# Two-layer spectral and MLP mixer on one core: fewer opening matmuls, a gate ahead of a GpSimd step, and a rewritten order of layer 2

## The chip, the core and the metric

The kernel runs on one core of a Trainium2 chip. The core's engines work side by side, each through its own queue in order: TensorE (PE, matmuls; its weight loads are listed as PEld), VectorE (DVE), ScalarE (ACT), GpSimd (POOL) and SyncE (SP, which here only starts DMAs). They wait for one another through semaphores. Matmuls write to PSUM, which has eight banks of 128 x 512 fp32; DVE or ScalarE have to evict a result before its bank can be written again. The metric is device time in microseconds (us); lower is better.

## What is computed

```python
def reference(x, w_r, w_i, w1, w2, w3, w4):      # names shortened, B = 1, S = 2048, D = 512, F = 1792
    for _ in range(2):                           # the same two blocks twice
        x = x + A(layernorm(x))
        x = x + Bk(layernorm(x))
    return x

def A(x):                                        # global filter
    X = rfft2(x)                                 # over S and D
    return irfft2(X * (w_r + 1j * w_i), s=(S, D)).astype(bf16)

def Bk(x):                                       # spatial shift + MLP
    h = gelu(layernorm(x) @ w1)
    # quarter c of the columns is shifted by -1, +1, -2, +2 rows, zeros moving in
    x1 = x + shift(h) @ w2
    return x1 + gelu(layernorm(x1) @ w3) @ w4
```

Everything is bf16 in and out, with fp32 sums.

## The kernel before

The 2048 rows are split as s = 16 p + q: p on the 128 partitions, q as sixteen row blocks of 128 x 512. The whole state x stays in SBUF. The two-dimensional FFT is done as small matrix products, in this sequence: over p (`over_p`, with a table T that is scaled per row block by the layer norm's 1/std, called Tq), over the columns d (`over_d`), over q (`over_q`, with the table TL), then the product with the filter W (`weigh`, on DVE), and back over q (`back_q`, with the table TR), d (`back_d`) and p (`back_p`). The q transforms of the sixteen frequency groups b need TL in two forms, of which only the first is loaded; the second is made on the chip by swapping and negating columns (`turn_TL`, L227, two GpSimd operations for each half of the table). W is loaded for half of the partitions and doubled by DMAs from SBUF to SBUF (L183); TR's third plane is a negated copy of its first (`negate`, L759, on DVE).

The order of all work is written out by hand, as strings of short codes: ORDER_0 for the first p transforms, ORDER_A for layer 1 and ORDER_B for layer 2. Each code issues the instructions of one step, and each engine runs its share in the order in which the codes stand. A number after the dot is the PSUM bank. In the layers:

- d, t: d transform and its eviction to TV; q, x: q transform and its eviction to X; p: the product with W
- b, m: back over q and its eviction to hT; D, Y: back over d and its eviction; P, a: back over p and the add into x, with a row sum
- s, r, e, i, c, n: squares, statistics and the normalizing of rows for the MLP; T: the DMA transpose of two row blocks (SP queue)
- v, h: w1 matmuls and gelu; u, f: w2 matmuls and the add of the shifted rows; k, R, o: second norm; U: its DMA transposes
- w, g: w3 matmuls and gelu (ScalarE, 128 x 1024 at a time); W, A: w4 matmuls of a row block (14 of them) and the add into x; y: the store of a row block (SP queue)
- a letter V or A after the number of t, x, m, Y, n or o says whether DVE or ScalarE does it.

In ORDER_0, Q scales T for a row block (letter V: DVE, A: ScalarE), O is a p transform of one or two row blocks, and G its eviction to V. The row blocks come in the order 2, 3, 0, 1, 6, 7, 4, 5, 10, 11, 8, 9, 13, 12, 14, 15; the last tables are Q13V Q12V, Q14V and Q15A.

At the very start PE runs WAKE matmuls on a tile of zeros (`wake`, L241, `fill`, L252) while x is loaded; a few more zero matmuls stand between the first p transforms (FILL). `load_rest` (L179) is called once after ORDER_0 has been issued and fills GpSimd's queue: the loads of FA, TL and half of TR, the first doubling of W, the turn of TL's first half, the second doubling, the turn of the second half, two more doublings, and the other half of TR. Nothing in it waits for the p transforms. `load_mlp` (L199) puts the loads of the MLP weights on SP's queue; its first DMA reads what the last doubling wrote.

Layer 2 ends with the stores. In layer 1 one row block (row 14 of the order, `columns`, L688) has its w4 matmuls, add and statistics done in two column halves of 256, numbered 14 and 24; all other row blocks, and all of layer 2's, are done in one piece of 512 columns. `store` (L707) writes whole row blocks.

The instructions go out through a framework that places each engine's waits from the tiles that are read and written; the order strings are kept as they stand.

Of the kernel before, what the change touches and what calls it, by code (L numbers as in the profile page):

```python
# [13 lines left out]
BF16 = dt.bfloat16  # L14
# [4 lines left out]
D = 512  # L19
# [134 lines left out]
def load_all(K, A_x, A_w_r, A_w_i, B_w1, B_w2, B_w3, B_w4):  # L154
    nc = K.nc
    tabs = dft_tables()
    dram = {k: nc.inline_tensor(v, name="tab_" + k).ap() for k, v in tabs.items()}

    def table(k, eng):
        t = K.const.tile(list(tabs[k].shape), BF16, name=k)  # L160
        eng.dma_start(t[:], dram[k])
        setattr(K, k, t)

    K.x = K.big.tile([P, NQ, D], BF16, name="x_state")
    xv = A_x[0].rearrange("(p q) d -> p q d", q=NQ)
    table("T", nc.scalar)
    for h in range(8):
        nc.sync.dma_start(K.x[:, h * 2:h * 2 + 2, :], xv[:, h * 2:h * 2 + 2, :])
    K.W = K.const.tile([P, 2, NH, 257], BF16, name="W")
    planes = [w.rearrange("(m j) f -> m j f", j=64) for w in (A_w_r, A_w_i)]  # L170
    for pl, v in enumerate(planes):
        nc.scalar.dma_start(K.W[2::4, pl, 0], v[:, 32])
    for lo in range(0, NH, 8):
        for pl, v in enumerate(planes):
            load_W(K, v, pl, lo, lo + 8)
    K.TL = K.const.tile([P, 2, NB, P], BF16, name="TL")
    K.TR = K.const.tile([P, 3, NH, 64], BF16, name="TR")

    def load_rest():  # L179
        q = nc.gpsimd  # L180
        load_TL = lambda k: q.dma_start(K.TL[:, 0, 8 * k:8 * k + 8], dram["TL"][:, 8 * k:8 * k + 8])
        load_TR = lambda k: q.dma_start(K.TR[:, 0:2, 16 * k:16 * k + 16], dram["TR"][:, :, 16 * k:16 * k + 16])
        double = lambda k: q.dma_start(K.W[1::2, :, 8 * k:8 * k + 8], K.W[0::2, :, 8 * k:8 * k + 8])  # L183
# [12 lines left out]
    K.load_rest = load_rest
    K.load_G2 = lambda: nc.sync.dma_start(K.G[:], dram["G2"])

    def load_mlp():  # L199
        gate2 = K.const.tile([1, 16], BF16, name="gate2")  # L200
        nc.sync.dma_start(gate2[:], K.W[1:2, 1, NH - 1, 1:17])
        for k in ("G", "Tinv"):
            table(k, nc.sync)
        for k, w, n, c in (("w1", B_w1, 4, D), ("w2", B_w2, 4, D), ("w3", B_w3, 4, FH), ("w4", B_w4, 14, D)):
            t = K.const.tile([P, n, c], BF16, name=k)
            nc.sync.dma_start(t[:], w.rearrange("(t p) n -> p t n", p=P))
            setattr(K, k, t)

    K.load_mlp = load_mlp
    K.eps = K.const.tile([P, 1], FP32, name="eps")  # L210
    nc.vector.memset(K.eps[:], EPS)
    K.eps2 = K.const.tile([P, 1], FP32, name="eps2")
    nc.gpsimd.memset(K.eps2[:], EPS * EPS)
    K.mhalf = K.const.tile([P, 4], FP32, name="mhalf")
    nc.gpsimd.memset(K.mhalf[:], -0.5)
# [11 lines left out]
def turn_TL(K, sl):  # L227

    old, new = [K.TL[:, k, sl].rearrange("p b (c h) -> p b c h", h=2) for k in range(2)]
    K.nc.gpsimd.tensor_scalar(new[:, :, :, 0], old[:, :, :, 1], -1.0, None, op0=ALU.mult)  # L230
    K.nc.gpsimd.tensor_copy(new[:, :, :, 1], old[:, :, :, 0])
# [9 lines left out]
def wake(K):  # L241
# [6 lines left out]
    K.zeros = t  # L248
    fill(K, WAKE)

# [120 lines left out]
def scaled_T(K, q, r, eng="V"):  # L371

    K.Tq[q] = K.stream.tile([P, 2, P], BF16, name="Tq", bufs=12)
    if eng in "VP":
        e = K.nc.vector if eng == "V" else K.nc.gpsimd
        e.tensor_scalar(K.Tq[q][:], K.T[:], r, None, op0=ALU.mult)
    else:
        K.nc.scalar.activation(K.Tq[q][:], K.T[:], ACT.Copy, bias=0.0, scale=r)
# [51 lines left out]
def first_front(K):  # L430

    new_V(K)
    K.Tq = {}
    at = {q: (g, i) for g, rows in enumerate(GROUPS) for i, q in enumerate(rows)}
    L = [Stats(K, n=len(rows)) for rows in GROUPS]
    for g, rows in enumerate(GROUPS):
        if any(q in ON_ACT for q in rows):
            L[g].sums()
    ps = {}

    def stats(q):
        g, i = at[q]
        if q in ON_ACT:
            L[g].mean(i, K.x[:, q, :])
            L[g].square(i, K.x[:, q, :])
        else:
            L[g].bn(i, K.x[:, q, :])

    def aggr(q):
        g, i = at[q]  # L450
        L[g].aggr(i)

    def scale(q, eng):
        g, i = at[q]
        scaled_T(K, q, L[g].r[:, i:i + 1], eng)

    def front(k):
        ps[k] = over_p(K, FIRST[k], k == len(FIRST) - 1)
        if k in FILL:
            fill(K, FILL[k])  # L460

    def take(k, eng):
        take_V(K, FIRST[k], ps[k], eng, k == len(FIRST) - 1)

    def means(g):
        for i, q in enumerate(GROUPS[g]):
            if q in ON_ACT:
                L[g].from_means(i)

    table = {"s": stats, "i": aggr, "f": means, "S": lambda g: L[g].std(),  # L470
             "J": lambda g: L[g].invert(), "p": lambda g: L[g].rstd(), "Q": scale, "O": front, "G": take}
    for op in ORDER_0.split():
        if op[0] in "QG":
            table[op[0]](int(op[1:-1]), op[-1])
        else:
            table[op[0]](int(op[1:]))
    K.load_rest()
    K.load_mlp()
    spare = K.grp.tile([P, 4, 4, P], BF16, name="xT", bufs=4)
    K.nc.sync.dma_start_transpose(spare[:, 0, 0:1], K.zeros[:])  # L480


def layer(K, last):
# [3 lines left out]
    nc = K.nc  # L487
# [114 lines left out]
    def rstd2(g):  # L602
        ln[g].from_sums()
        ln[g].rstd_twice(g in ROOT)
        if g not in ROOT:
            ln[g].shift()
# [80 lines left out]

    def columns(n):  # L688

        if last or n % 10 != 4 or n < 14:  # L690
            return n, slice(0, D)
        return 14, slice(0, D // 2) if n == 14 else slice(D // 2, D)

    def w4(n):
        r, d = columns(n)
# [9 lines left out]
        nc.vector.tensor_tensor(x, ps.pop(("W", n)), x, op=ALU.add)  # L705

    def store(n):  # L707
        nc.sync.dma_start(K.out_v[:, ROWS[n], :], K.x[:, ROWS[n], :])

    def stats4(n):  # L710
        r, d = columns(n)
# [73 lines left out]
            table[op[0]](int(op[1:]))  # L785


WAKE = 44
FILL = {0: 3, 1: 3, 2: 2, 3: 2, 4: 2}
GROUPS = [[0, 1, 2, 3], [4, 5, 6, 7], [8, 9, 10, 11], [12, 13], [14, 15]]  # L790
ON_ACT = [1, 5]
FIRST = [[0, 1], [2, 3], [4, 5], [6, 7], [8, 9], [10, 11], [12, 13], [14], [15]]
UNITS = {b: [b, b + 1] if 2 <= b < 14 else [b] for b in (0, 1, 2, 4, 6, 8, 10, 12, 14, 15)}
ROOT = (0, 1)
LATE = ((14, 15), (0, 14))
TAKE_B = ("FFFFFFFFFFFFFFFB", "FFFFFFFFFFFFFFFB")
ROWS = [*range(2, 16), 0, 1]
# [26 lines left out]
G6A G14A X4.5 X3.4 L6  # L824
"""
ORDER_B = """
d4.0 d1.3 d8.6 t4A q4.0 t1A q1.2 t8A x4V d15.5 t15A p4 d12.6 x1A p1 t12A d10.4 q15.0 x15A p15 t10A q8.2 x8V q12.6 x12A
d2.0 t2A d0.4 d14.5 b1.3 m1A q10.0 t0A q2.6 t14A p8 b8.3 x2A m8A d6.4 t6A p12 x10V b5.2 m5A p2 b12.1 m12A p10 b13.0
q0.4 m13V q6.6 x0A x6A q14.2 b4.1 m4A p0 b10.4 b11.5 p6 x14A m11A m10A b3.6 m3A b9.0 b0.1 m0A p14 m9V b7.2 m7V b2.7
b14.4 m14A b6.5 m2V b15.2 m6A m15V m15A D3.6 Y3A D2.0 Y2A D1.4 Y1A P6.6 a6 P4.1 P7.7 a4 s6 P5.5 a7 s4 D0.3 s7 a5 s5  # L830
D5.0 Y0V Y5A r1 e1 P3.6 a3 s3 P1.4 a1 i1 n6V s1 P0.7 a0 P2.6 a2 P10.2 P11.5 n7A D4.3 n5V s0 T3 s2 D6.0 n4V T2 D7.6 Y4V
Y6A P8.4 P13.1 r0 e0 Y7A a10 s10 i0 n0A n3V n2V T1 n1V a13 P12.3 P9.2 P14.7 a9 a11 s13 s9 a8 P15.0 a15 s11 s8 v2.1
v3.5 h3 a14 a12 r2 n10V h2 s15 T0 v1.4 h1 n11V n9V v0.6 T5 n8V u3.2 c1 f3 h0 u1.5 s12 u0.0 s14 c0 T4 f1 u2.7 v5.1 f0
E0 k0 r3 n12V k1 n13V v4.4 n15V n14V f2 h5 k3 u4.6 f4 h4 k2 u7.2 c2 f7 E3 R0 o3A u5.5 f5 u6.3 k7 T6 T7 E7 v6.4 h6 o0V
E2 E1 o1V U0 o2V U1 v7.6 h7 u13.1 k4 u12.2 E5 c3 f13 k13 f6 u15.6 E6 f15 u14.0 f12 E12 w5.3 g5 f14 k14 k12 E14 u11.2
f11 w2.6 w1.0 g1 k15 R3 g2 w3.4 w6.0 g3 u9.6 g6 f9 E15 w0.4 w4.6 g0 u8.2 E13 k5 o15V f8 E8 u10.4 f10 g4 W2.7 W1.4 k6
E10 o13V A2 o14A U7 R1 o12A U6 o6V E4 k11 W0.2 A0 A1 o5V k9 o4V U2 W3.0 A3 w26.3 g26 k10 w22.0 g22 w27.2 o7V y1 w21.5
w24.0 E11 g21 z0 y3 E9 g24 k8 R2 w23.6 g23 g27 o10V U3 w12.0 g12 o9V w25.4 g25 W13.3 A13 w10.0 g10 W12.6 A12 w8.4 o8V
W15.7 U4 g8 A15 w9.3 y12 g9 o11V U5 W14.0 w7.1 g7 w19.3 g19 w13.6 A14 y2 w17.4 g17 w11.0 g11 g13 W6.5 A6 y0 W4.7 A4
W5.0 A5 y13 w20.5 W7.4 g20 w14.2 g14 A7 w15.4 y4 g15 w16.0 g16 w18.5 g18 W9.2 A9 y7 W8.3 A8 W11.4 y15 A11 W10.7 A10 y5  # L840
y6 y14 y11 y9 y8 y10
"""


# [28 lines left out]
```

## Time and profile before

| | us |
|---|---|
| median of five runs (lowest to highest) | 349.68 (349.25 to 350.26) |
| the profiled run | 349.87 |
| its span from first to last instruction | 348.1 |
| PE busy in the span | 337.1 |
| ScalarE busy | 197.3 |
| DVE busy | 185.7 |
| GpSimd busy | 62.2 |

Most numbers in this text come from the timeline of one profiled execution, whose times count from the span's start. A row gives start, length, engine, line, operation, output and inputs, shapes, and a count where several equal instructions stand in a row; in brackets, idle time of the engine before it and what ended it. Lengths run from the start to the last write, and a following instruction of the same engine usually starts a little before that. A matmul's end is modelled: matmuls of 256 columns are listed with 0.27 us but follow each other every 0.109 us, and those of 512 columns every 0.216 us.

Where PE stands in the kernel, by its timeline: the zero matmuls from 1.01 us, the first p transform at 7.26, the first d transform at 18.82, layer 1's back transforms from about 30, layer 2's first d transform at 185.03, its D stage at 204.70, its w1 matmuls from 219.37, and the last w4 matmul just before the last add at 344.02.

### The profile page before, as it was taken

The numbers are of one execution on the slowest core, as the hardware profiler recorded it, in microseconds if no ns is written. First come the engines' busy times: TensorE is split into PE (matmuls) and PEld (weight loads), VectorE is DVE, ScalarE is ACT, GpSimd is POOL, SyncE is SP. The second block draws the span as 40 slices with busy tenths as digits, with TensorE's granted clock in tenths as the row PEclk, the third lists the DMA queues.
The fourth block names the chain that finished last, engine by engine and source line by source line (L and its number), as shares of the span: only waits on it lengthen the run. The fifth ranks groups of instructions, "written<-read, shape, count | busy, mean of one in ns | idle before, by whom it ended". The sixth has DMA issues, their size and how long they took to land. (4 is left out here: it accounts for less than half of the span.)

```text
span 348.1 us, 5562 instructions
## 1 busy us (share of the span) xinstructions
PE 337.1 (97%) x2110; PEld 188.7 (54%) x2129; DVE 185.7 (53%) x444; ACT 197.3 (57%) x350; POOL 62.2 (18%) x157
## 2 busy tenths in 40 slices
PE   8899999999999999999999999999999999999995
PEld 6668885444444444445577888544444444444442
DVE  5989597568424417844786969767343201102011
ACT  5969999864803706424528989985581372150410
POOL 2560046422200003200100002463130010000000
PEclk9999999999999999999999999999999999999999
DMA  7987956303030110400000002454003400400201
GB/s 245 289 291 216 370 159 118 74 19 61 1 62 0 28 34 0 90 2 0 1 2 0 2 2 43 82 107 77 0 2 60 90 0 15 108 0 17 75 0 60
DMA packets 45129, 24.38 MB, mean 70 GB/s; under 512 B 34928, under 2 KB 42096, under 8 KB 45104
## 3 DMA queue, kind: packets, MB, share of 16 engines
q1 hardware_dynamic: 43760, 20.00, 23.0%
q0 software_dynamic: 1104, 3.94, 3.2%
q8 instruction: 16, 0.26, 0.3%
q10 hardware_dynamic: 240, 0.10, 0.1%
q14 instruction: 9, 0.07, 0.1%
HBM read 11.41 MB, written 2.10 MB: 39 GB/s over the span
## 5 line engine op out<-in xcount | busy, mean ns | idle before, releaser
L686 ACT ACTIVATE gT<-ps 128x1024 bf16<-128x1024 f32 x56 | 56.4, 1022 | 103.3 <-PE ps L679 102.9
L679 PE MATMUL ps<-xT,w 128*128 128x512 bf16 x448 | 99.8, 379 | 0.2 <-DMA xT<-xn 0.2
L699 PE MATMUL ps<-w,gT 128*128 128x512 bf16 (+1 forms) x448 | 97.8, 372 | 0.6
L705 DVE TENSOR_TENSOR x_state<-ps,x_state 128x512 bf16<-128x512 f32 (+1 forms) x33 | 22.0, 674 | 97.7 <-PE ps L699 93.8
L699 PEld LDWEIGHTS <-gT 128*128 128x128 bf16 x462 | 45.1, 98 | 51.3
L679 PEld LDWEIGHTS <-w 128*128 128x128 bf16 x448 | 43.6, 98 | 52.8 <-issue 0.9
L652 DVE SCALAR_TENSOR_TENSOR xn<-xn,ln_c,ps 128x512 bf16<-128x512 bf16 x32 | 23.3, 744 | 25.0 <-PE ps L644 9.3
L644 PE MATMUL ps<-w,hT 128*128 128x512 bf16 x123 | 28.8, 379 | 0.3
L628 PE MATMUL ps<-xT,w 128*128 128x512 bf16 x128 | 28.6, 379 | 0.0
L596 DVE SCALAR_TENSOR_TENSOR x_state<-ps,x_state 128x512 bf16<-128x512 f32 x32 | 20.4, 685 | 7.1 <-PE ps L588 7.0
L282 ACT ACTIVATE junk<-xn 128x512 bf16<-128x512 bf16 x32 | 19.9, 622 | 5.9 <-DVE xn L652 5.7
L270 DVE BATCH_NORM_STATS2 ln_st<-x_state 128x6 f32<-128x512 bf16 (+1 forms) x31 | 20.0, 665 | 3.7 <-DMA x_state<-in_A_x_dram 3.5
L644 PEld LDWEIGHTS <-hT 128*128 128x128 bf16 x128 | 12.5, 98 | 15.4 <-ACT hT L635 0.4
L547 DVE TENSOR_TENSOR PB<-X,W 128x2048 bf16<-128x2048 bf16 (+1 forms) x20 | 20.2, 1050 | 0.5 <-ACT X L151 0.4
L628 PEld LDWEIGHTS <-w 128*128 128x128 bf16 x128 | 12.4, 98 | 14.9 <-issue 0.6
L282 ACT ACTIVATE xn<-x_state 128x512 bf16<-128x512 bf16 x32 | 20.0, 630 | 0.4
L635 ACT ACTIVATE hT<-ps 128x512 bf16<-128x512 f32 x32 | 17.6, 605 | 3.2 <-PE ps L628 2.9
L288 POOL TENSOR_SCALAR ln_mv<-ln_s 128x4 f32<-128x4 f32 x16 | 4.3, 269 | 77.1 <-DVE x_state L596 66.4
L151 ACT ACTIVATE TV<-ps 128x1024 bf16<-128x1024 f32 (+1 forms) x15 | 14.4, 981 | 3.6 <-PE ps L504 2.3
L504 PE MATMUL ps<-FA,V 128*128 128x256 bf16 x128 | 16.0, 273 | 0.3 <-ACT V L151 0.2
L305 POOL TENSOR_SCALAR ln_ve<-ln_mv 128x4 f32<-128x4 f32 x11 | 3.3, 302 | 71.8 <-DVE ln_mv L298 71.1
L576 PE MATMUL ps<-G,hT 128*128 128x256 bf16 x128 | 15.3, 273 | 0.8 <-ACT hT L151 0.4
(86 smaller groups left out, 392.1 us busy)
## 6 DMA issues: line engine op xcount, KB each, us to landing
w<-in_B_w_dram SPq DMA_DIRECT2D x2, 1792.0 KB, 13.8
W<-W POOLq DMA_DIRECT2D x4, 514.0 KB, 4.5
x_state<-in_A_x_dram SPq DMA_DIRECT2D x8, 256.0 KB, 5.2
out_dram<-x_state SPq DMA_DIRECT2D x16, 128.0 KB, 1.9
TR<-tab_TR POOLq DMA_DIRECT2D x2, 512.0 KB, 6.3
w<-in_B_w_dram SPq DMA_DIRECT2D x2, 512.0 KB, 5.8
W<-in_A_w_r_dram SPq DMA_DIRECT2D x7, 128.5 KB, 7.0
W<-in_A_w_i_dram SPq DMA_DIRECT2D x7, 128.5 KB, 6.6
```

Source lines behind the costliest of these rows:

```text
L270: self.K.nc.vector.bn_stats(self.st[i][:, int(k)], src)
L282: K.nc.scalar.activation(out, src, ACT.Square, bias=0.0, scale=D ** -0.5, accum_out=self.s[:, i, 1:2])
L547: nc.vector.tensor_tensor(t, X.pop(u)[:, 0:2 * n].unsqueeze(1).to_broadcast([P, 2, 2 * n, 256]), K.W[:, :, 2 * u:2 * u + 2 * n, 1:257], op ...
L596: nc.vector.scalar_tensor_tensor(K.x[:, q, :], ps.pop(("P", q)), 1.0, K.x[:, q, :], op0=ALU.mult, op1=ALU.add, accum_out=ln[g].s[:, i, 0:1])
L628: nc.tensor.matmul(o[:, i], lhsT=K.w1[:, t, j * P:(j + 1) * P], rhs=xT[g][:, :, t, :], start=(t == 0), stop=(t == 3))
L635: nc.scalar.activation(hv[:, 2 * h + i, 4 * g:4 * g + 4, PAD:PAD + P], o[:, i].rearrange("p (q c) -> p q c", q=4), ACT.Gelu_apprx_tanh, bi ...
L644: nc.tensor.matmul(o, lhsT=K.hT[:, j, st:st + P], rhs=K.w2[:, j, :], start=(j == 0), stop=(j == 3))
L652: nc.vector.scalar_tensor_tensor(xn[:, q, :], xn[:, q, :], ln[q // 4].c[:, q % 4:q % 4 + 1], ps.pop(("u", n)), op0=ALU.mult, op1=ALU.add, ...
L679: nc.tensor.matmul(o[:, i], lhsT=K.w3[:, c, t * P:(t + 1) * P], rhs=xT3[g][:, :, c, :], start=(c == 0), stop=(c == 3))
L686: nc.scalar.activation(gT[g][:, 2 * j:2 * j + 2, :], ps.pop(("w", k)), ACT.Gelu_apprx_tanh, bias=0.0, scale=1.0)
L699: nc.tensor.matmul(o, lhsT=gT[g][:, t, i * P:(i + 1) * P], rhs=K.w4[:, t, d], start=(t == 0), stop=(t == 13))
L705: nc.vector.tensor_tensor(x, ps.pop(("W", n)), x, op=ALU.add)
```

## The change

Four things change.

1. WAKE goes from 44 to 35.
2. `load_rest` takes the last scaled table as an argument, and GpSimd copies two elements of it to a small tile before it turns the first half of TL. As the queue is in order, everything behind that copy starts after the last table (row block 15's) has been written.
3. `columns` now halves one row block in each layer, HALVES = (14, 10): row 14 in layer 1 as before, row 10 in layer 2, numbered 10 and 20. `store` stores a half when it is given one.
4. ORDER_B is another string throughout. It contains the same steps, with W20, A20 and y20 added, in another sequence, with other banks, and with other engines for some evictions: t1 and x15 move from ScalarE to DVE; of the m, DVE has 10, 11, 14 and 7 instead of 13, 9, 7 and 2; Y3 and Y4 are on DVE instead of Y0 and Y4; n7 is on DVE instead of ScalarE; of the sixteen o steps, ten change their engine. The last w4 steps are W10.5, W9.7 and W20.0.

```diff
-    def load_rest():
+    def load_rest(after):
...
         double(0)
+        gate = K.const.tile([1, 2], BF16, name="gate")
+        q.tensor_copy(gate[:], after[0:1, 0, 0:2])
         turn_TL(K, slice(0, 8))
         double(1)
...
     def scale(q, eng):
+        nonlocal last_T
         g, i = at[q]
         scaled_T(K, q, L[g].r[:, i:i + 1], eng)
+        last_T = K.Tq[q]
...
-    K.load_rest()
+    K.load_rest(last_T[:])
...
     def columns(n):
-        if last or n % 10 != 4 or n < 14:
+        if n not in (HALVES[last], HALVES[last] + 10):
             return n, slice(0, D)
-        return 14, slice(0, D // 2) if n == 14 else slice(D // 2, D)
+        return HALVES[last], slice(0, D // 2) if n == HALVES[last] else slice(D // 2, D)
...
     def store(n):
-        nc.sync.dma_start(K.out_v[:, ROWS[n], :], K.x[:, ROWS[n], :])
+        r, d = columns(n)
+        nc.sync.dma_start(K.out_v[:, ROWS[r], d], K.x[:, ROWS[r], d])
...
-WAKE = 44
+WAKE = 35
...
+HALVES = (14, 10)
...
 ORDER_B = """
-d4.0 d1.3 d8.6 t4A q4.0 t1A q1.2 t8A x4V d15.5 t15A p4 d12.6 x1A p1 t12A d10.4 q15.0 x15A p15 t10A q8.2 x8V q12.6 x12A
-d2.0 t2A d0.4 d14.5 b1.3 m1A q10.0 t0A q2.6 t14A p8 b8.3 x2A m8A d6.4 t6A p12 x10V b5.2 m5A p2 b12.1 m12A p10 b13.0
-q0.4 m13V q6.6 x0A x6A q14.2 b4.1 m4A p0 b10.4 b11.5 p6 x14A m11A m10A b3.6 m3A b9.0 b0.1 m0A p14 m9V b7.2 m7V b2.7
-b14.4 m14A b6.5 m2V b15.2 m6A m15V m15A D3.6 Y3A D2.0 Y2A D1.4 Y1A P6.6 a6 P4.1 P7.7 a4 s6 P5.5 a7 s4 D0.3 s7 a5 s5
-D5.0 Y0V Y5A r1 e1 P3.6 a3 s3 P1.4 a1 i1 n6V s1 P0.7 a0 P2.6 a2 P10.2 P11.5 n7A D4.3 n5V s0 T3 s2 D6.0 n4V T2 D7.6 Y4V
...
-W5.0 A5 y13 w20.5 W7.4 g20 w14.2 g14 A7 w15.4 y4 g15 w16.0 g16 w18.5 g18 W9.2 A9 y7 W8.3 A8 W11.4 y15 A11 W10.7 A10 y5
-y6 y14 y11 y9 y8 y10
+d4.5 t4A d1.3 d8.1 t1V t8A q4.6 x4V q1.3 x1A p1 d15.5 t15A d12.2 t12A d10.6 t10A p4 q15.0 x15V p15 q8.4 q12.2 x12A x8V
+d2.6 t2A b5.1 d14.3 t14A b1.0 p12 m1A m5A d0.2 t0A q10.6 p8 q2.3 x10V p10 x2A d6.0 t6A b13.2 m13A p2 b4.3 q0.4 x0A p0
+q14.6 m4A q6.0 b10.2 m10V x14A x6A b12.5 b8.4 b2.3 m12A p14 b9.6 p6 m9A b11.7 m2A b3.1 b14.5 m3A m11V m14V b0.0 m0A
+m8A b7.3 m7V b6.2 b15.0 m6A m15A m15V D3.6 Y3V D2.0 Y2A D1.2 Y1A P6.6 P4.7 a6 D0.0 s6 Y0A a4 s4 P7.5 a7 s7 P5.4 a5 s5
+r1 P3.6 a3 P2.1 P0.2 s3 P1.3 a2 s2 a0 e1 s0 a1 s1 D7.6 D5.0 Y5A D4.4 i1 n6V n7V T3 D6.2 n5V Y6A n4V T2 Y4V P11.1 r0
+a11 e0 i0 P10.0 Y7A s11 n0A n3V P9.4 n2V n1V P12.3 T1 a9 s9 P8.5 a10 s10 P13.7 a8 P15.1 P14.2 s8 r2 a13 v2.4 h2 a15
...
+W0.5 W1.0 k9 o12V E6 A2 o7A o14V o15A U7 A0 k10 o13A U6 k8 A1 y1 R2 o11V E10 o4V o5A o6A W3.6 o10V w25.1 g25 w23.4 g23
+w22.2 g22 U2 U3 w13.0 y0 g13 A3 w27.6 g27 w26.3 g26 o9V w24.0 g24 w21.2 g21 w11.0 W15.7 A15 E8 o8A g11 w9.2 W14.5 A14
...
+z0 A9 y4 y5 y9 y6 W20.0 A20 y8 y20
 """
```

On the engines' queues this gives: PE nine zero matmuls fewer and fourteen matmuls more in the last w4 row (28 of 256 columns for 14 of 512); GpSimd one small copy more; DVE one add of 256 columns more; SP one store more.

More of the change, by code (lines that the diff above doesn't have):

```diff
@@ L439, in first_front @@
     ps = {}
+    last_T = None
     def stats(q):
@@ L832 @@
[L832 to L836, printed above, removed]
@@ L837 @@
-E10 o13V A2 o14A U7 R1 o12A U6 o6V E4 k11 W0.2 A0 A1 o5V k9 o4V U2 W3.0 A3 w26.3 g26 k10 w22.0 g22 w27.2 o7V y1 w21.5
-w24.0 E11 g21 z0 y3 E9 g24 k8 R2 w23.6 g23 g27 o10V U3 w12.0 g12 o9V w25.4 g25 W13.3 A13 w10.0 g10 W12.6 A12 w8.4 o8V
-W15.7 U4 g8 A15 w9.3 y12 g9 o11V U5 W14.0 w7.1 g7 w19.3 g19 w13.6 A14 y2 w17.4 g17 w11.0 g11 g13 W6.5 A6 y0 W4.7 A4
-W5.0 A5 y13 w20.5 W7.4 g20 w14.2 g14 A7 w15.4 y4 g15 w16.0 g16 w18.5 g18 W9.2 A9 y7 W8.3 A8 W11.4 y15 A11 W10.7 A10 y5
-y6 y14 y11 y9 y8 y10
+d4.5 t4A d1.3 d8.1 t1V t8A q4.6 x4V q1.3 x1A p1 d15.5 t15A d12.2 t12A d10.6 t10A p4 q15.0 x15V p15 q8.4 q12.2 x12A x8V
@@ new lines @@
+s15 T0 v3.6 h3 a12 a14 n9V n8V c0 v1.1 n11V h1 n10V s12 c1 v0.3 u3.2 h0 u0.7 s13 T5 u1.4 u2.0 s14 r3 c2 f3 f1 f0 T4
+n12V n15V k0 k1 n14V T7 v5.1 n13V T6 f2 v4.5 h5 h4 u4.4 u7.6 u6.0 u5.5 f7 k3 E2 k2 E0 v6.6 R0 o2V f6 E3 o0A o3V v7.2
+h6 E1 o1V h7 u12.1 u13.6 U1 c3 f13 f12 f4 k4 k6 k12 u14.7 u9.2 f14 k14 U0 E7 f9 u11.0 f5 w5.3 g5 E9 w3.1 E14 g3 w1.5
+g1 k5 u10.7 f11 w4.4 E4 f10 w2.1 k7 g2 E5 w0.6 g0 g4 w6.1 g6 u15.6 f15 R1 k15 k11 E15 u8.5 f8 W2.4 k13 R3 E12 E11 E13
+W0.5 W1.0 k9 o12V E6 A2 o7A o14V o15A U7 A0 k10 o13A U6 k8 A1 y1 R2 o11V E10 o4V o5A o6A W3.6 o10V w25.1 g25 w23.4 g23
@@ L842 @@
+w22.2 g22 U2 U3 w13.0 y0 g13 A3 w27.6 g27 w26.3 g26 o9V w24.0 g24 w21.2 g21 w11.0 W15.7 A15 E8 o8A g11 w9.2 W14.5 A14
+w10.0 g10 g9 W13.5 W12.1 A12 U4 A13 U5 y15 w7.3 g7 w19.6 g19 w15.1 g15 w8.4 w12.1 g8 g12 W6.6 A6 w17.2 g17 W7.0 y13
+y12 y14 W4.3 A7 w20.4 g20 w18.6 g18 w14.4 y3 w16.6 g16 g14 W5.0 A5 y7 W8.4 A4 W11.2 A11 y11 W10.5 A10 y10 W9.7 y2 A8
+z0 A9 y4 y5 y9 y6 W20.0 A20 y8 y20
 """
```

## The prediction

> **What bounds the kernel now.** I read the head of the page first, then TensorE's (PE's) timeline for its gaps, then the timelines of the engines that end those gaps.
>
> ```profile
> span 348.1 us, 5562 instructions
> PE 337.1 (97%) x2110; PEld 188.7 (54%) x2129; DVE 185.7 (53%) x444; ACT 197.3 (57%) x350; POOL 62.2 (18%) x157
> PE   8899999999999999999999999999999999999995
> ```
>
> PE is busy almost everywhere, so a saving counts only where PE waits now: the first 25 us, the FFT part of layer 2 (185 to 219 us), and what follows the last matmul. From 230 to 344 us PE is busy 113.34 of 114.00 us. Each place has its own limit. The front first (DVE, then GpSimd, then ScalarE and PE):
>
> ```profile
> 15.25 0.84 DVE L376 TENSOR_SCALAR Tq<-T,ln_r 128x256 bf16<-128x256 bf16 x2
> 16.26 0.87 DVE L376 TENSOR_SCALAR Tq<-T,ln_r 128x256 bf16<-128x256 bf16 x1
> 17.98 1.02 DVE L149 CAST V<-ps 128x512 bf16<-128x512 f32 x2 [0.30 <-PE ps L391]
> 18.92 0.42 DVE L762 TENSOR_SCALAR TR<-TR 128x1024 bf16<-128x1024 bf16 x1
> 21.31 0.69 DVE L149 CAST X<-ps 128x512 bf16<-128x512 f32 x1 [0.98 <-PE ps L528]
> 22.04 2.13 DVE L547 TENSOR_TENSOR PB<-X,W 128x1024 bf16<-128x1024 bf16 x2
> ...
> 15.37 1.69 POOL L230 TENSOR_SCALAR TL<-TL 128x512 bf16<-128x512 bf16 x1 [2.27 <-DMA TL<-tab_TL]
> 16.98 0.77 POOL L231 COPY TL<-TL 128x512 bf16<-128x512 bf16 x1
> 20.13 0.66 POOL L183 DMA_DIRECT2D W<-W  x1 [2.39 <-DMA W<-in_A_w_r_dram]
> ...
> 16.43 0.50 ACT L378 ACTIVATE Tq<-T,ln_r 128x256 bf16<-128x256 bf16 x1
> ...
> 16.23 0.27 PE L389 MATMUL ps<-Tq,x_state 128*128 128x256 bf16 x1 [0.37 <-DMA W<-in_A_w_i_dram]
> ```
>
> Two scaled tables took 0.48 us at 6.92, with GpSimd quiet; with its turn running, two take 0.84 and one 0.87. PE's waits at 16.23 and 17.28 end just after those tables (16.09, 17.13), so I put them down to DVE, not to the W DMA that the row names. In layer 2:
>
> ```profile
> 188.04 1.22 DVE L149 CAST X<-ps 128x1024 bf16<-128x1024 f32 x1 [2.34 <-PE ps L528]
> 191.55 0.69 DVE L547 TENSOR_TENSOR PB<-X,W 128x1024 bf16<-128x1024 bf16 x1 [0.41 <-ACT X L151]
> 204.70 2.78 PE L576 MATMUL ps<-G,hT 128*128 128x256 bf16 x24 [0.39 <-DVE hT L149]
> 211.75 2.34 PE L588 MATMUL ps<-Y,Tinv 128*128 128x256 bf16 x20 [0.30 <-DVE Y L149]
> 344.02 0.69 DVE L705 TENSOR_TENSOR x_state<-ps,x_state 128x512 bf16<-128x512 f32 x1 [2.26 <-remote]
> ```
>
> DVE and ScalarE both run without a gap from about 192 to 204.5 us and end together; PE waits for them at 204.70, and for a Y eviction at 211.75. The last line is the tail: one add after the last matmul, then a store.
>
> **Nine zero matmuls fewer.** Warm, they follow each other every 0.109 us, so 35 end 9 x 0.109 = 0.98 us earlier, at 6.28 instead of 7.26. The first table is ready at about 6.92 + 0.24 = 7.2, so PE waits there: 0 to 0.1 us gained, I take 0. The cover lost is PE's warmth over a 0.9 us pause; PE pauses 1.18 us at 10.07 now with the granted clock still 1.00 after it, so 0 there too. If the clock did fall, about 13 matmuls at the cold 0.213 us of the start, 1.4 us, less the 0.5 us of waits behind it: up to 0.9 lost.
>
> **The turn waits for the last table.** The tiny copy on GpSimd waits for row 15's table (ScalarE, 16.43 + 0.50 = 16.93). Its own price, about 0.2 us, is that of GpSimd's small operations (0.19 to 0.25). What it frees, step by step: row 12's table ends at 15.73 instead of 16.09; the reciprocal after it and row 14's table end at 16.24 instead of 17.13; PE starts rows 12 and 13 at 15.80 instead of 16.23, eight matmuls to 16.67, rows 14 and 15 to 17.54 (16.98 for row 15's table is no limit), the four fills to 17.98. The evictions to V follow: the last DVE one ends at 18.35 instead of 19.00. The d transforms lose their wait, and q0 starts at about 20.14 instead of 20.81: 0.66 us.
> Not all of it survives. The first product p0 needs X (now 22.00, then 21.33) and the doubled W; the first doubling is issued at 12.47 and the slowest of the four lands 9.1 us after its issue, 21.56. So p0 starts at about 21.62 instead of 22.04: 0.42 us, and from there DVE has no gap over 0.1 us until 39.4, so what p0 gains the stage gains.
> Queued behind the copy on GpSimd are the turn's two operations, now about 17.2 to 19.65; the second doubling, which waited 2.39 us for W until 20.13 anyway, so 0.48 us of cover is left; the second turn, the other doublings and TR's second half, unmoved, and with them the SP copy that waits for the last doubling. q0, at 20.14, needs the turned table at 19.65. But DVE's negation of TR, now at 18.27 instead of 18.92, falls under the turn. Row 14's table lost 0.63 us that way; the negation may lose 0 to 1.4 (to the turn's end). At 0.63 it ends near 19.3, DVE's TV eviction then starts 0.3 earlier than its 19.60, and q0 still waits only for PE. So the bounds are 0 and 0.66, taken 0.42.
> The Trainium skill, SBUF — State Buffer, "Who interferes with whom", speaks against this: DVE and GpSimd hold their shared port for a whole instruction and the other blocks fully. Here row 12's table, started under the turn, ended at 16.08, a microsecond before that operation did, while row 14's did wait to its end. By the rule the negation starts only at 19.65, DVE's TV eviction follows to 20.7, q0 starts at 20.75 and the front gains 0.06, an estimate; the sum would be -0.11 instead of the -0.47 below.
>
> **The new order of layer 2.** The same 64 d, 64 q, 128 b, 64 D and 64 P matmuls, with DVE taking t1 and x15 from ScalarE. I followed PE, DVE and ScalarE through the new order with the rows' durations (casts 1.14 and 0.60 issue to issue on DVE, 0.92 and 0.48 on ScalarE, products 1.14 and 0.60), and each bank's last reader. t1 falls into DVE's 2.34 us of idle before 188.04, so it is free; x15 costs 0.60, of which the 0.41 wait at 191.55 pays most. DVE ends its hT evictions within 0.1 us of now, and D3 starts at 204.66 to 204.8 instead of 204.70. Then Y3 goes to DVE and Y0 to ScalarE: the wait at 211.75 goes. But ScalarE now runs s6 Y0 s4 s7 s5 s3 s2 e1 s0 s1 ahead of Y5: from 208.76, eight squares at 0.61, one cast 0.92 and e1 0.22 make 214.78, so Y5 is there at 215.80 and P11 waits 0.5 to 0.6 from 215.25. v2 starts at 219.4 as now, its second bank waits about 0.13 for a8's add, and the u's wait for h0 a little more. Sum +0.15, bounds -0.3 (both waits gone) and +0.75 (below).
> Behind 230 us I followed the transposes: SP issues U1, U0 at about 239.2 and 240.5; at 3.2 us each they land by 243.7, w5 starts at 244.9. U7 and U6 have 2.8 us to spare. U2 and U3 now stand behind the store y1, which waits for W1's add at 269.6; with 0.44 for the store and 1.25 a transpose they land by 274.5, w13 starts at 276.8. Cost 0.
>
> **Row 10's halves.** 28 matmuls at 0.109 for 14 at 0.216: +0.03. The last add is 128x256, 0.42 us (layer 1's two) instead of 0.69: -0.27. Two stores for one; y8 stands ahead of the last store, and SP issues at 0.44 each: y9, y6, y8 from 343.1 end at 344.45, about when the half's add ends, so +0.05. Net -0.2, between -0.35 and 0.
>
> **Sum.** 0 - 0.42 + 0.15 - 0.20 = -0.47. The profiled run took 349.87 (span 348.1 and 1.77 around it), which makes 349.4; it stands 0.19 above the median of 349.68, so the median goes to 349.2.
>
> **Rivals.** A, more is gained: the doubling lands in time, so the front keeps 0.66, and layer 2 loses its wait at P11 (-0.1), -0.2 at the tail: -0.96, 348.7. For it: 0.66 is what PE's own rows give. Against: the 9.1 us landing.
> B, slower: DVE becomes layer 2's bound. It takes 0.60 + 0.60 us more, and if neither idle hides it, the hT evictions end 1.2 late: -0.42 - 0.20 + 1.2 + 0.15 = +0.73, 350.4. It decides against the change from 0.5 us of uncovered DVE work on. For it: DVE has no gap from 192.16 to 204.55. Against: the 2.34 us.
> C, the wait does not free the front, since the turn meets the negation instead: 0 there, -0.05 in all, 349.6.
>
> **Numbers.** Forecast 0.38, A 0.33, B 0.20, C 0.09. This kernel's measurement tells about 0.2%, 0.70 us, from no change. The forecast's own range is 348.8 to 349.6, a quarter of it below 348.98. Faster: 0.33 + 0.10 = 0.43; slower 0.20; same 0.37. Range 348.3 (both gains at their bounds) to 350.4 (B).
>
> **What would show it.** Right: the last three DVE tables at 0.24 to 0.29 each, PE without a wait at rows 12 to 14, V done near 18.4, p0 near 21.6; layer 2's D at the same distance from its first d (19.7 us); a wait of about 0.5 before P11; a last add of 0.42. Wrong: PEclk below 1.00 before 20 us, the negation above 1 us, q0 waiting for GpSimd, D3 later than 20.2 us after d4, or a PE wait anywhere behind w5.

## The result, and the profile after

The changed kernel takes 350.54 us (median of 37 runs, 349.27 to 352.19) beside 349.73 for the kernel before on the same chips (63 runs, 349.02 to 350.80). The ratio is 1.0022, with a 95% interval of 1.0014 to 1.0029: slower by about 0.8 us, where 0.5 less was forecast. The profiled execution took 350.54, its span is 348.8 (before: 349.87 and 348.1). Line numbers of the changed kernel are higher by 2 in the front and by 6 in the layers (L376 is now L378, L628 is L634).

The front first, as VectorE's and GpSimd's timelines show it:

```profile
15.48 0.48 DVE L378 TENSOR_SCALAR Tq<-T,ln_r 128x256 bf16<-128x256 bf16 x2
16.16 0.29 DVE L378 TENSOR_SCALAR Tq<-T,ln_r 128x256 bf16<-128x256 bf16 x1
18.63 0.80 DVE L769 TENSOR_SCALAR TR<-TR 128x1024 bf16<-128x1024 bf16 x1
21.74 2.37 DVE L553 TENSOR_TENSOR PB<-X,W 128x1024 bf16<-128x1024 bf16 x2
```

```profile
17.23 0.17 POOL L190 COPY gate<-Tq 1x2 bf16<-1x2 bf16 x1 [3.77 <-ACT Tq L380]
17.49 1.66 POOL L232 TENSOR_SCALAR TL<-TL 128x512 bf16<-128x512 bf16 x1
19.96 0.67 POOL L183 DMA_DIRECT2D W<-W  x1
20.66 1.67 POOL L232 TENSOR_SCALAR TL<-TL 128x512 bf16<-128x512 bf16 x1
```

The tables are as quick as forecast, and the first product p0 starts at 21.74 instead of 22.04. But p0 and p1 take 2.37 us together, as the second turn (20.66 to 22.32) runs beside them, so they end at 24.11 instead of 24.16. Of the 0.30, 0.05 is left. The kernel before had this meeting too: its 2.13 us for the two products lie beside a second turn that started at 20.83.

The loss sits in layer 1, at a place that the forecast doesn't mention. TensorE's timeline there:

```profile
51.90 2.34 PE L594 MATMUL ps<-Y,Tinv 128*128 128x256 bf16 x20 [0.16 <-DVE x_state L602]
54.92 1.46 PE L634 MATMUL ps<-xT,w 128*128 128x512 bf16 x6 [0.67 <-DMA xT<-xn]
```

In the kernel before the same two rows read 51.96 and 54.14, and the second has no wait:

```profile
51.96 2.34 PE L588 MATMUL ps<-Y,Tinv 128*128 128x256 bf16 x20 [0.16 <-DVE x_state L596]
54.14 2.10 PE L628 MATMUL ps<-xT,w 128*128 128x512 bf16 x9
```

The first w1 matmul (v2) waits for T3's DMA transpose. It was issued at 49.34 us (before: 49.40), but lands 4.62 us after that instead of 3.27. The view of the DMAs shows why it is late. First the changed kernel from 50 to 54 us in 40 slices (the digits are the busy share of the DMA engines in tenths; below them GB/s, and the packets by queue):

```profile
DMA  0000028999999900000000000000999999999999
GB/s 0 0 0 0 0 44 182 212 207 200 197 333 64 18 0 0 0 0 0 0 8 8 10 8 10 10 10 8 187 279 294 287 262 287 289 287 292 289 292 289
q1 hardware_dynamic: 1867, 0.47, 108.2%
q8 instruction: 1, 0.02, 1.4%
```

Then the kernel before from 49.5 to 53.5, in which queue q8 moves nothing:

```profile
DMA  0000000000059999999999973279999999999941
GB/s 0 0 0 0 0 0 0 0 0 0 0 108 212 228 228 210 202 230 197 215 197 215 192 126 59 54 174 218 228 212 189 220 210 195 218 207 187 195 87 31
q1 hardware_dynamic: 2110, 0.52, 68.6%
```

Before, the transpose's packets follow one another to the end. In the changed kernel they run for 0.6 us, then one packet of 16 KB of the kind "instruction" starts at 51.10 and takes 0.93 us (the slice with 333 GB/s), and for the 1.4 us from 51.4 to 52.8 hardly anything moves. Before, that packet came at 49.12, 0.28 ahead of the transpose's issue.

Layer 2 and the tail, TensorE first:

```profile
205.72 2.78 PE L582 MATMUL ps<-G,hT 128*128 128x256 bf16 x24 [0.45 <-ACT hT L151]
216.77 3.65 PE L594 MATMUL ps<-Y,Tinv 128*128 128x256 bf16 x32 [0.41 <-ACT Y L151]
...
345.19 0.42 DVE L711 TENSOR_TENSOR x_state<-ps,x_state 128x256 bf16<-128x256 f32 x1 [0.84 <-PE ps L705]
```

The first d of layer 2 starts at 185.97 instead of 185.03, so D3 stands 19.75 us behind it, as against 19.67. The difference of the two executions, followed through: -0.05 in the front, +0.83 at v2, +0.16 at the first w3 (its transposes land a little later), +0.23 from layer 2's first d to the last add, -0.28 from the last add's start to the last store's landing, -0.22 behind it. Sum +0.67, the difference of the spans. The last of these terms is no gain of the change: what follows the last landing took 1.38 to 1.60 us in fourteen executions of all these kernels.

### The profile page after: what moved, and what is told of

Same layout as the page of the kernel before. It is cut to its first block, busy times and chain, and to the rows that moved or that the text cites. A ratio compares the mean times of both kernels' runs of the same rounds, so it can differ in the third digit from the quotient of the medians.

```text
span 348.8 us, 5584 instructions
## 1 busy us (share of the span) xinstructions
PE 336.4 (96%) x2116; PEld 189.1 (54%) x2134; DVE 185.7 (53%) x444; ACT 199.0 (57%) x351; POOL 62.5 (18%) x158
## 4 chain that ended last, share of the span: by engine, by line
PE 76%; ACT 9%; DVE 7%; DMA 4%; issue 2%; SPq 1%; DVEq 0%; ACTq 0%
PE ps L685 28%; PE ps L705 27%; PE ps L634 8%; PE ps L650 6%; PE ps L510 3%; ACT hT L151 2%; DMA xT<-xn 2%; ACT V L151 2%; DMA x_state<-in_A_x_dram 2%; DVE PB L553 2%; PE ps L582 2%; DVE x_state L602 1%; ACT xn L284 1%; ACT X L151 1%; PE ps L594 1%
## 5 line engine op out<-in xcount | busy, mean ns | idle before, releaser
L705 PEld LDWEIGHTS <-gT 128*128 128x128 bf16 x476 | 46.5, 98 | 50.1
L634 PE MATMUL ps<-xT,w 128*128 128x512 bf16 x128 | 28.7, 379 | 0.7 <-DMA xT<-xn 0.7
L634 PEld LDWEIGHTS <-w 128*128 128x128 bf16 x128 | 12.4, 98 | 15.8 <-issue 1.4
L370 ACT ACTIVATE xn<-xn,ln_mr,ln_r 128x512 bf16<-128x512 bf16 x15 | 11.9, 806 | 9.3 <-DVE x_state L665 5.0
L564 PE MATMUL ps<-TR,PB 128*128 128x128 bf16 x256 | 15.9, 219 | 0.2 <-ACT X L151 0.2
```

The lines of the kernel that those rows point to most:

```text
L634: nc.tensor.matmul(o[:, i], lhsT=K.w1[:, t, j * P:(j + 1) * P], rhs=xT[g][:, :, t, :], start=(t == 0), stop=(t == 3))
L705: nc.tensor.matmul(o, lhsT=gT[g][:, t, i * P:(i + 1) * P], rhs=K.w4[:, t, d], start=(t == 0), stop=(t == 13))
```

## The experiments

Theory F (fetch): the packets of queue q8 are TensorE's code. There are 16 or 17 of them in an execution, and between the first and the last of the kernel before lie 3,743 of TensorE's matmuls and weight loads, 250 a packet on the mean. Nine zero matmuls fewer are 18 instructions fewer, so each later packet falls at a later place of the work. Theory G: the wait on GpSimd changes the order of the transfers and makes the transposes late. Theory W: the shorter warm-up costs clock.

**The changed kernel with 44 zero matmuls again** (e1_wake44)

```diff
-WAKE = 35
+WAKE = 44
```

> The changed kernel with 44 zero matmuls again instead of 35; the wait for the last table, layer 2's new order and row 10's halves stay. In the trace of the changed kernel a 16 KB packet of the 'instruction' kind, 0.93 us long, falls at 51.10 us into the packets of T3's transpose, which then lands 4.62 us after its issue instead of 3.27, and TensorE waits 0.83 us at v2; before, that packet came at 49.12. Theory F (fetch): TensorE's code is fetched 256 instructions at a time, so 18 instructions fewer (nine matmuls, nine weight loads) move each fetch later. With 44 the packet is back at 49.0 to 49.6, T3 lands about 3.3 us after its issue, v2 waits under 0.2, and the time is about 0.8 below the changed kernel's 350.54: 349.6 to 349.9, ratio 0.999 to 1.001. Theory G (the wait on GpSimd, which starts the later transfers in another order, makes the transposes late): T3 still lands 4.6 after its issue, 350.4 to 350.7. Theory W (the shorter warm-up leaves a lower clock in part of the runs): about 349.9, but the packet's place and T3's landing do not matter.

Measured 350.08 us (12 runs), ratio 1.0004 (0.9993 to 1.0016). The packet is at 49.91, 0.54 ahead of T3's issue at 50.45; T3 lands 3.24 us after it, and v2 doesn't wait. G falls. The time came down by 0.46, not by 0.8: the median is just above the range that F gave.

**The kernel before with 35** (e2_before35)

```diff
-WAKE = 44
+WAKE = 35
```

> The kernel before with 35 zero matmuls instead of 44, nothing else. Theory F: the packet moves into T3's transpose (50.5 to 51.5), T3 lands over 4 us after its issue, v2 waits about 0.8, and the time is 350.4 to 350.8 against 349.7, ratio 1.002 to 1.003. Theory G: T3 lands 3.3 after its issue as before and the time stays at 349.6 to 349.9. Theory W: slower by 0 to 0.5 in the median, with the granted clock below 1.00 in a tenth or more of the runs, and T3 as before.

Measured 352.09 us (6 runs), ratio 1.0066 (1.0045 to 1.0087): 2.4 more, over twice what F expected. The packet is at 50.14, 1.46 behind T3's issue, T3 takes 4.38 and v2 waits. And there is a second wait in layer 2. TensorE's timelines of both places:

```profile
54.44 1.89 PE L628 MATMUL ps<-xT,w 128*128 128x512 bf16 x8 [0.86 <-DMA xT<-xn]
...
238.46 1.90 PE L628 MATMUL ps<-xT,w 128*128 128x512 bf16 x8 [1.21 <-DMA xT<-xn]
```

The transpose for the second of these was issued at 233.49 and landed 4.92 us later; a fetch packet started at 236.41. The new order of layer 2 issues its transposes at other times, and in the changed kernel the packet (at 238.60) meets none that is waited for. So the change holds the nine matmuls' second loss off, by its other part.

**35 at the start, nine more behind the second p transform** (e3_moved9)

```diff
-FILL = {0: 3, 1: 3, 2: 2, 3: 2, 4: 2}
+FILL = {0: 3, 1: 12, 2: 2, 3: 2, 4: 2}
```

> The changed kernel with its 35 zero matmuls at the start, and nine more behind the second p transform (12 there instead of 3), where TensorE waits 1.64 us for x: as many instructions as with 44, but the short warm-up stays. Theory F: the packet is back at about 49, T3 lands about 3.3 us after its issue, v2 waits under 0.2, 349.6 to 349.9. Theory W: the warm-up is as short as in the changed kernel, so it stays at 350.2 to 350.7 (the nine fill a wait, which could warm the clock, but only after 10 us). Theory G: 350.4 to 350.7.

Measured 349.98 us (12 runs), ratio 1.0003 (0.9990 to 1.0016). The packet is 0.65 ahead of T3's issue, T3 takes 3.25, no wait at v2. The warm-up is as short as in the changed kernel, so W falls as the cause of the 0.5. It isn't without any effect: of the 68 executions with 35 zero matmuls at the start (four kernels) five show a granted clock of 0.993 to 0.995, at 351.29 to 352.84 us, and of all others with a clock on record none is below 0.997. Four of the five are of the changed kernel; without them its median is 350.52 instead of 350.54.

**44 at the start, nine fewer in the fills** (e6_fewer_fills)

```diff
-WAKE = 35
-FILL = {0: 3, 1: 3, 2: 2, 3: 2, 4: 2}
+WAKE = 44
+FILL = {0: 1, 1: 1, 2: 1}
```

> The changed kernel with the full 44 zero matmuls at the start, and nine fewer of the zero matmuls that fill the waits between the p transforms (1, 1, 1, 0, 0 behind the first five groups instead of 3, 3, 2, 2, 2): as many instructions on TensorE as the changed kernel, but the long warm-up. Theory F: the fetch packet falls at 50.5 to 51.5 into T3's transpose, which lands over 4 us after its issue, v2 waits 0.8 to 1.0, and the time is as the changed kernel's, 350.3 to 350.9. Theory W (the warm-up's length decides): as e1_wake44, 349.9 to 350.2, T3 landing 3.2 to 3.3 us after its issue.

Measured 350.57 us (12 runs), ratio 1.0024 (1.0013 to 1.0034), the changed kernel's own time. The packet is at 50.92 and TensorE waits as in the changed kernel. Its timeline at v2, and the DMAs from 50 to 54 us:

```profile
54.89 1.46 PE L634 MATMUL ps<-xT,w 128*128 128x512 bf16 x6 [0.86 <-DMA xT<-xn]
```

```profile
DMA  0002899999990000000001000002999999999999
q8 instruction: 1, 0.02, 1.7%
```

The halt is the same. With the third experiment this is the clean pair: the place of the nine matmuls makes no difference, their number does.

**40 instead of 44, in the kernel before** (e9_before40)

```diff
-WAKE = 44
+WAKE = 40
```

> The kernel before with 40 zero matmuls instead of 44: eight instructions fewer on TensorE, against 18 with 35. In the traces so far the fetch packet is harmless where it falls before T3's transpose is issued or up to 0.3 us behind it (before: 0.28 ahead of the issue) and delays it by 1.1 to 1.5 us where it falls 1.4 to 1.8 us behind the issue. Theory F: here it falls 0.4 to 0.8 us behind the issue, and is 0.9 long, so it still overlaps the transpose's first packets: T3 lands 3.6 to 4.6 us after its issue and the time is 350.0 to 352.0, over the kernel before and under e2_before35 (352.09). Theory W (the length of the warm-up): 349.7 to 350.2 with T3 at 3.2 to 3.3. No effect at all would put the edge of the collision between 0.6 and 1.4 us.

Measured 351.58 us (6 runs), ratio 1.0053 (1.0037 to 1.0069). The packet falls 1.16 behind T3's issue, a little later than expected. T3 takes 4.31, v2 waits 0.69, and layer 2 has its second wait again (1.1 for the transposes). Four matmuls cost 1.80 us (351.58 against 349.78 for the kernel before beside it), nine 2.39, and the two intervals overlap: it is not a price for each matmul, but a collision that happens or not.

**53 instead of 35, in the changed kernel** (e10_wake53)

```diff
-WAKE = 35
+WAKE = 53
```

> The changed kernel with 53 zero matmuls: 18 instructions more than the kernel before, not fewer. Theory F: the packet falls at 47 to 48.3, a microsecond and more before T3's issue; T3 lands 3.2 to 3.3 us after its issue, v2 does not wait, 349.9 to 350.2 as e1_wake44 (350.08), if no other fetch falls into a transpose (then 0.5 to 1.5 more, to be seen as a landing over 4.3). The fills now end at 8.2 us, 0.9 past the first table, but the third p transform waits for x until about 11.3 anyway: 0. Theory W (a longer warm-up is better): below e1_wake44 by 0.2 or more.

Measured 350.53 us (12 runs), ratio 1.0017 (1.0004 to 1.0029). T3 is as F had it (3.33, no wait), but the time is 0.3 above the range, as long as the changed kernel's. My price of 0 for the longer fills may be what was wrong; that rests on one execution and isn't shown. In it 25 of the zero matmuls went at the cold 0.213 us, the fills end at 9.53, and the first p transform starts at 9.36, two microseconds later than in most others. Two later transposes of layer 1 land 4.62 and 4.84 us after their issue (packets at 98.66 and 126.45 fall into them), and nobody waits for them. So more instructions can move a packet into a transpose just as fewer can.

**The wait of GpSimd alone, in the kernel before** (e4_gate_only)

```diff
+        gate = K.const.tile([1, 2], BF16, name="gate")
+        q.tensor_copy(gate[:], after[0:1, 0, 0:2])
         turn_TL(K, slice(0, 8))
...
```

> The kernel before with only the wait of GpSimd's turn for the last table (44 zero matmuls, the old order of layer 2, row 14 alone in halves). As the forecast had it: 0.42 less, about 349.3, with q0 near 20.2 and p0 near 21.6 at 1.02 us as before. What the changed kernel's trace shows instead: q0 0.3 earlier, p0 0.3 earlier but 1.76 long instead of 1.02, since the second turn runs beside it, so that 0.06 is left at the fifth q: 349.6 to 349.8, ratio 0.999 to 1.001. Theory G: T3 lands over 4 us after its issue and the time is about 350.4.

Measured 350.17 us (12 runs), ratio 1.0005 (0.9994 to 1.0016): not the 349.3 of the forecast. Its profiled execution did gain 0.4 up to the first b transform (28.89 against 29.30), 0.12 of it as the last row's statistics started earlier (14.28 against 14.40). But q0 is at 20.16, p0 waits for the doubled W (0.58, until 21.85), and its products are long again:

```profile
21.93 1.83 DVE L553 TENSOR_TENSOR PB<-X,W 128x1024 bf16<-128x1024 bf16 x2 [0.58 <-DMA W<-W]
```

**Layer 2's order and row 10's halves, without the wait** (e5_order_only)

```diff
-WAKE = 35
+WAKE = 44
-        q.tensor_copy(gate[:], after[0:1, 0, 0:2])
```

> The kernel before with only layer 2's new order and row 10's halves (44 zero matmuls, no wait of GpSimd for the last table). The forecast had -0.05 for these two (+0.15 and -0.20). The traces with the new order so far show TensorE 159.18 us from layer 2's first d to the last matmul against 158.73 (+0.45), and 3.65 from there to the end of the span against 4.34 (-0.69): by these rows -0.24, so 349.4 to 349.6, ratio 0.9990 to 1.0000. If the wait on GpSimd gives what it was meant to give, this kernel is 0.3 to 0.4 slower than e1_wake44, which has the wait as well (350.08); if the wait costs (theory C of the forecast, or worse), it is faster than that by 0.2 to 0.6.

Measured 350.05 us (12 runs), ratio 1.0004 (0.9990 to 1.0018); e1_wake44, with the wait, took 350.08. Neither alternative holds: the wait makes no difference here, and the two edits of layer 2 come out at +0.35 where I expected -0.24. The interval takes in no change at all, so the sign of the 0.35 isn't shown by this run alone.

**The halves alone** (e7_halves_only)

```diff
+HALVES = (14, 10)
...
-... W10.7 A10 y5 y6 y14 y11 y9 y8 y10
+... W10.7 A10 W20.0 A20 y5 y6 y14 y11 y9 y8 y10 y20
```

> The kernel before with only row 10, the last row of layer 2, in column halves (the first half in its old place, the second right behind it, its own store last): the old order of layer 2, 44 zero matmuls, no wait on GpSimd. By the traces the halves take 0.65 to 0.69 off the time from the last matmul to the end and add 0.03 of matmuls, and the 0.45 that the new order adds on TensorE is not there: 349.0 to 349.2, ratio 0.9980 to 0.9986. The forecast's price for the halves was -0.20: 349.5. If the gain of the tail comes from the new order's stores and not from the halves: 349.6 to 349.8.

Measured 349.52 us (12 runs), ratio 0.9991 (0.9978 to 1.0003), on the forecast's -0.20 more than on the -0.65. So the new order, and not the halves, costs: 350.05 - 349.52 = 0.53, with an uncertainty nearly as large.

**The halves with the wait** (e8_gate_halves)

```diff
         load_TR(0)
         double(0)
+        gate = K.const.tile([1, 2], BF16, name="gate")
+        q.tensor_copy(gate[:], after[0:1, 0, 0:2])
```

> e7_halves_only with the wait of GpSimd's turn for the last table added. The forecast's price of the wait is -0.42; the trace of e4_gate_only has the fifth q and all behind it 0.4 earlier, that of the changed kernel only 0.06, and the medians of e4_gate_only (350.17) and of the kernel before it (349.70) say +0.2 to +0.5. So the difference to e7_halves_only is -0.4 by the forecast, 0 by the changed kernel's trace, and +0.3 if the wait, which holds GpSimd until about 17 us, costs in most executions: then the second turn runs beside the first products and the later doublings start late.

Measured 349.67 us (12 runs), ratio 0.9999 (0.9988 to 1.0011): +0.15 to the kernel without the wait, less than their intervals can tell apart. The forecast's -0.4 would show.

**The changed kernel without the wait** (e11_order35)

```diff
-        q.tensor_copy(gate[:], after[0:1, 0, 0:2])
```

> The changed kernel without the wait of GpSimd (35 zero matmuls, the new order, row 10's halves): e5_order_only (350.05) with nine zero matmuls fewer. Theory F: T3 lands over 4.2 us after its issue, v2 waits 0.8 to 1.0, 350.4 to 350.8, so the price of the nine is 0.4 to 0.7 with the wait and without it. If the nine are only harmful together with the wait: 350.0 to 350.2. If the wait costs what e4_gate_only and e8_gate_halves show (0.1 to 0.4), this kernel is 0.1 to 0.4 faster than the changed one (350.54).

Measured 350.44 us (12 runs), ratio 1.0019 (1.0009 to 1.0029). T3 lands 4.81 us after its issue, v2 waits 1.18. So the nine matmuls cost 0.39 without the wait (350.44 - 350.05) and 0.46 with it (350.54 - 350.08), and the wait costs 0.10 here.

**The cut at column 384** (e12_quarter)

```diff
-        return HALVES[last], slice(0, D // 2) if n == HALVES[last] else slice(D // 2, D)
+        cut = CUT[last]
+        return HALVES[last], slice(0, cut) if n == HALVES[last] else slice(cut, D)
...
+CUT = (256, 384)
```

> e7_halves_only (349.52) with row 10 cut at column 384 instead of 256: the last add and the last store hold 128 columns. By the rows the last add took 0.69 us at 512 columns and 0.42 at 256, so about 0.29 at 128; the last store landed 1.76 us after its issue at 512 and 1.54 at 256, so about 1.43. Sum -0.24: 349.2 to 349.4, ratio to the kernel before 0.9980 to 0.9990. If the last store's landing is a fixed time below 256 columns, -0.13: 349.4. If the first part's add (0.55) now stands in the way of the last one, nothing is gained: 349.5.

Measured 349.08 us (12 runs), ratio 0.9984 (0.9973 to 0.9994), just below the range, and 0.44 below the halves alone where 0.24 was expected. This one beats both kernels: 0.70 below the kernel before, in the old order, with 44 zero matmuls and no wait on GpSimd. VectorE's timeline of the tail:

```profile
342.97 0.56 DVE L710 TENSOR_TENSOR x_state<-ps,x_state 128x384 bf16<-128x384 f32 x1 [1.51 <-PE ps L704]
343.82 0.29 DVE L710 TENSOR_TENSOR x_state<-ps,x_state 128x128 bf16<-128x128 f32 x1 [0.29 <-PE ps L704]
```

The first part's add is over 0.29 us before the second may start, and the last store lands 1.44 us after its issue.

## Why the prediction was wrong, point by point

The price of each part, by medians of kernels that differ in that part alone:

| part | forecast | measured (differences of two medians, us) |
|---|---|---|
| nine zero matmuls fewer | 0 | +0.46, +0.39 in the new order; +2.39 in the old |
| turn waits for the last table | -0.42 | +0.47, +0.15, +0.03, +0.10 |
| layer 2's new order | +0.15 | +0.53 without the wait, +0.41 with it |
| row 10's halves | -0.20 | -0.18 without the wait, -0.50 with it |

Added up along one path (halves, order, wait, nine fewer): -0.18 + 0.53 + 0.03 + 0.46 = +0.84, against 349.70 (these runs' median before) and 350.54. Each of these medians of 12 runs is uncertain by some 0.4 us, so none of the prices of the wait is clear of zero by itself, while the -0.42 of the forecast would have shown. The price of the nine is firmer when the kernels with the new order are taken together: 350.05 for the three whose packet falls ahead of T3's issue (e1_wake44, e3_moved9, e5_order_only; 36 runs) and 350.54 for the three where it falls into T3 (the changed kernel, e6_fewer_fills, e11_order35; 61 runs), a difference of 0.5 with a 95% interval of 0.2 to 0.7. The exception is e10_wake53, at 350.53 without this collision.

**"Nine zero matmuls fewer ... I take 0": this step failed.** Both of its statements on the clock and on the first table held in the profiled execution (its granted clock stays 1.00; TensorE waits for the table from 6.3 on). But it costed the matmuls only as time at the start. They are also 18 instructions, and the packets that bring TensorE's code share the DMA engines with the transposes. Over the fourteen profiled executions: in nine the packet starts between 1.14 us ahead of T3's issue and the issue itself, and T3 lands after 3.21 to 3.33 us; in five it starts 1.16 to 1.79 us behind the issue, and T3 lands after 4.31 to 4.81, with TensorE waiting 0.67 to 1.18. No execution falls between. From the first b transform to layer 2's first d the five take 156.69 to 157.22 us, the nine 155.70 to 156.05. The other transposes say the same: eight of them, in three executions (e2_before35, e9_before40, e10_wake53), have such a packet 1.1 to 2.9 us behind their issue, and they land after 4.18 to 5.03. That the packet causes the halt is shown as far as moving it by other instructions moves the halt with it; why one packet of 0.9 us stops the transpose for longer than that is not shown. The price by the times (0.5) is less than these stages differ by (0.9 on the mean). Each kernel has one trace, so it isn't known whether every execution of it has the collision, and whether the nine give part of the price back at the start stays open too (see the end).

**The wait of the turn, -0.42.** Its first links held: the tables at 0.28 to 0.29, TensorE without a wait at row 12, the evictions to V ending at 18.71 where 18.35 was forecast, in an execution whose x came 0.24 later. Two links failed. First, "the second doubling, which waited 2.39 us for W until 20.13 anyway": that was one execution. In three of the seven executions without the wait W was there early enough for an issue at 18.67 to 18.86. GpSimd's timeline of one of them (the halves alone):

```profile
14.17 1.66 POOL L230 TENSOR_SCALAR TL<-TL 128x512 bf16<-128x512 bf16 x1 [0.62 <-DMA TL<-tab_TL]
15.76 0.83 POOL L231 COPY TL<-TL 128x512 bf16<-128x512 bf16 x1
18.73 0.66 POOL L183 DMA_DIRECT2D W<-W  x1 [2.14 <-DMA W<-in_A_w_i_dram]
19.42 1.66 POOL L230 TENSOR_SCALAR TL<-TL 128x512 bf16<-128x512 bf16 x1
```

and VectorE's in the same execution:

```profile
21.83 1.30 DVE L551 TENSOR_TENSOR PB<-X,W 128x1024 bf16<-128x1024 bf16 x2
```

There the second turn is over before the products, and p0 and p1 take 1.30 to 1.37 together; in the other four without the wait it isn't, and they take 1.89 to 2.34. In the seven executions with the wait the first turn ends at 19.69 to 21.61, the second starts between 20.31 and 22.23, and the two products take 1.83 to 2.37. Second, "what p0 gains the stage gains" forgot that. The other stated limit, the doubling's landing 9.1 us after its issue, was no limit in the changed kernel's execution (20.03), but it was in two others (21.85, 23.19). From the start of the last row's statistics on VectorE (14.40 in the kernel before) to the first b transform the three with the early second doubling take 13.67 to 14.00 us and the other four without the wait 14.53 to 14.90; with the wait six take 14.36 to 14.61 and one, whose W came late, 15.92. The median is 14.53 in both groups: the wait gains some 0.2 where the second turn runs beside the products anyway, and gives away more where it would have been over. Also, the slow tables that the step was built on are plain in only three of the seven executions without the wait.

The Trainium skill, SBUF — State Buffer, "Who interferes with whom", was set against this part, with a full block where rows seemed to overlap. The negation fits it: under the turn it ended 0.28 us after the GpSimd operation that it met (19.15 and 19.43), and 0.28 again where that operation ended at 19.40 and 19.68 followed; in all seven executions with the wait it is 0.28 or 0.29. The estimate of q0 by that rule, 20.75, was too late all the same (20.51), since it held the negation back to the end of both GpSimd operations: it ended while the second ran. The products fit the same reading only in part. In the changed kernel p0, 0.69 long alone, ended 0.51 after the copy of the second turn (22.99 and 23.50). But in six other executions p0 took its 0.69 wholly inside the turn's first operation (e3_moved9: 22.30 to 22.99 inside 21.40 to 23.07), and row 12's table in the kernel before ended inside such an operation as well, so a full block isn't what every row shows, and here the measurement decides.

**Layer 2, +0.15.** The mechanism was right: D3 19.75 us behind the first d (19.63 to 19.77 was forecast), the wait before P11 0.57 from issue to issue, 0.41 in the row above, which counts from a modelled end (0.5 to 0.6), v2's second bank 0.15 (0.13), no wait behind w5. TensorE takes 159.23 us from the first d to the last add with the new order and the halves, 159.09 with the old order and the halves: +0.14. What was mis-sized is the stores, "+0.05". From the last add's start to the last store's landing the new order takes 2.20 us and the old 1.99, both with halves, as in the new order SP issues four stores in a row. The last add ends at 345.61, but SP, which issues y9, y6 and y8 at 344.38, 344.75 and 345.23, comes to its store at 345.77; the landing took 1.62 from there, beside 1.54. So +0.35 by the traces, and 0.41 to 0.53 by the times.

**Halves, -0.20.** Right in size by the times, though -0.18 and -0.50 are far apart; by the traces (halves alone against before) -0.38, of which +0.10 up to the last add and -0.48 from there to the last landing. The step left out that half a row also lands sooner: 1.54 us after its issue instead of 1.76.

**The rivals.** B's number was the nearest (350.4), but by luck: its mechanism didn't happen, as D3 was not late. C named the right part (the wait gains nothing) with the wrong meeting: the second turn and the products, not the first turn and the negation. A fell. The slower side, at 0.20, held only B; no case in it had a transfer delayed by something that no row of the kernel's own code shows. None of the forecast's signs of being wrong appears in the changed kernel's profile either: they all watch the front and layer 2, and the loss sits between them, in layer 1.

## What to carry to other kernels

Where TensorE waits for nothing but a transfer, count instructions as well as time: taking some out moves every later packet of code, and a DMA transpose that such a packet falls into can land over a microsecond late. Look for the "instruction" queue in the view of the DMAs around the transfers that are waited for, and try a few counts, in both directions. A cover read from one execution ("it waited until 20.13 anyway") is worth no more than that execution where a transfer sets it; with a start that differs from run to run, take both ends for it.

## What the runs showed of the hardware

Sixteen or seventeen packets of 16 KB (0.26 or 0.28 MB) bring TensorE's code during the run, each 0.9 to 1.4 us long as a rule, and when one falls into T3's transpose, its rate goes from some 200 GB/s to under 20 for 1.2 to 1.6 us (read off the slices of five executions). A late transpose alone is no proof of such a packet: in twelve of the fourteen executions one that is issued near 77 us lands after 3.93 to 4.31 us with no 16 KB packet in it, and what delays it is not shown.

The number of zero matmuls that went at the cold pitch of 0.213 us was 13 to 27 in fourteen executions, so 44 of them ended anywhere from 7.33 to 8.79 us. The Trainium skill, TensorE: Matmul & The Clock Gate, Part 1: The HAM clock gate, says that the count differs from run to run as the gate's window does not start with the kernel, which these runs agree with; its examples have 6, 11 and 14. Nine fewer would then start the first p transform earlier in some executions (7.05 to 7.55 with 35, 7.17 to 8.63 with 44); the times do not show a gain from it (e3_moved9 349.98, e1_wake44 350.08), and that stays open.
